# Convolution and expert layer in one kernel: the scatters at a sort's end spread, four tiles kept for them, and one stage with split rows

## The chip, the cores and the metric

One Trainium2 chip, one core. The metric is the device time of one execution in microseconds; the median of three runs is given. A profile of one execution stands beside them.

## The reference

```python
# x: (8, 5696, 128), h: (5696, 128); E = 8 experts, F = 1024
y = irfft(rfft(x, n=2*S, axis=1) * rfft(h, n=2*S, axis=0)[None], n=2*S, axis=1)[:, :S]
x = y.reshape(8 * 5696, 128)
logits = x @ w_gate                       # (45568, 8)
e = argmax(logits); gate = max softmax(logits)
for each expert e:
    out[rows of e] = gate * (relu(x[rows of e] @ w1[e]) @ w2[e])
```

A long convolution over the sequence for every channel, and then for each of 45568 tokens the one expert of eight that scores highest: 128 to 1024, relu, 1024 to 128, times its softmax weight. All in float32.

## The kernel before, in words

**The work.** The convolution is a Fourier transform in two factors (48 and 120 points) written as matmuls, and goes through three groups of batches: group 0 has 2 batches, groups 1 and 2 have 3 each. Each group passes three stages:

- Stage A (`steps_a`, `phase_a`): 120 x 512 blocks of x times a 120-point matrix; the result goes to the DRAM tensor U. With `A3[g]` true the rows are split first: `cut` makes a rounded copy on ScalarE (line 258) and the remainder on the engine that `ALO[g]` names (line 259), and each transform is three matmuls in the fast float32 kind in place of one in whole float32 (line 280).
- Stage B (`phase_b`), the filter: U by frequency, forward matmul `xp` (line 470), product with the filter on VectorE (495, 498), the sum `combine` (506, on POOL; for group 2's first `ALONE` = 20 steps on VectorE), inverse matmul `vp` (514), copy, store to V. 120 steps for a group.
- Stage C (`phase_c`), the last transform and the sort: `yp` (647) from V, rows to `rt` (662), transposes, logits, the choice of expert (`route`), the rank in its list (`rank`). Every column of 120 tokens then waits in the list `sorts` until `sort_one` sends it with one indirect DMA from POOL to its rows in the DRAM tensor SR (584), at most 8 in flight. 48 steps for group 1 and for group 2, three columns a step.

When a group's sort is done, `tables` works out on VectorE which tiles of 256 rows are complete, and the group's part of the expert layer may start (`moe`): part 0 has 37 tiles, part 1 67, part 2 the rest. A tile is read from SR (940; seven buffers `xr`), weights are read where the expert changes (961), and each of its four steps is layer 1 (992), relu on ScalarE (998) and its remainder on VectorE (1000), two steps later layer 2 (1012). The tile's rows are then delivered by two indirect DMAs from POOL (1035). The first row load of a part waits for the last scatters of its sort.

**The order.** Every engine and DMA queue runs its instructions in the order in which the program issues them. That order comes from generators: each yields a cost in ns, and `run` always continues the one whose sum of costs, divided by its share, is smallest. These costs only set the order. An expert step costs 1420; the rest (`rest`, all stages of groups 1 and 2) has the share 0.75. A filter step of group 2 costs 0.78 x 1280 = 998, a sort step of group 1 `RATE[2]` x 3150, one of group 2 `RATE[5]` x 3150.

While group 1 is sorted, group 2's stage A runs inside it as a guest (72 transforms, up to two for a sort step; `A3[2]` is false). Scatters are taken from `sorts` at `settle`, at `logit_out`, and by each relu of an expert step; whatever is left when the sort ends is sent at once.

A part whose sort had a guest isn't released by the sort, but in the next group's stage B, when that stage's costs exceed `HEAD`:

```python
for cost in phase_b(gr):
    spent += cost
    yield cost
    if spent > HEAD and wait:
        wait.pop().ready = True
```

Group 2's stage B begins with a yield of 6000. While no part is released, `experts` is held and the rest goes on alone.

Of the kernel before, what the change touches and what calls it, by code (L numbers as in the profile page):

```python
# [49 lines left out]
HOLD = (0, 0, 0)  # L50
AHEAD = 2
ALONE = 20
HEAD = 26000
A3 = (True, True, False)
ALO = ('gpsimd', 'vector', 'vector')
AT = 650
WARM = 7
# [2 lines left out]
LULL = (29000, 0.448)  # L60
RARE = 3
XR = 7
RATE = (0.372, 0.559, 0.45, 0.8, 0.78, 0.6)


@with_exitstack
def conv_moe(ctx: ExitStack, tc: tile.TileContext, I, out, B, S, D, E, F, split):
# [68 lines left out]
    for g, nbs in enumerate(split):  # L136
        gr = Group(g, b0, sum(nbs))
# [104 lines left out]
    def steps_a(gr, tag, bufs):  # L242
# [7 lines left out]
        xts, uts, xss = {}, {}, {}  # L250
        split = A3[g]

# [56 lines left out]
    def phase_a(gr):  # L309
        start, begin, store, flush, M = steps_a(gr, "six", SIX)  # L310
        half = AT if gr.g == 0 else 750 * RATE[3 * gr.g - 3]
        start()
# [10 lines left out]
    class Guest:  # L323
# [17 lines left out]
        def rest(self):  # L341
            while self.m < self.M:
                self.begin(2)
                yield 1500 * RATE[3 * self.gr.g - 3]
                self.end()
# [53 lines left out]
    def phase_b(gr):  # L399
# [117 lines left out]
        def save(n):  # L517
            q, c = items[n]
            qb, k0 = divmod(q, QB)
            if k0 == 0 and c == 0:  # L520
                outs_[qb] = sb.tile([K2, QB, gr.cols], F32, tag="six", name=f"vt{g}_{q}", bufs=SIX)
            nc.scalar.copy(outs_[qb][:, k0, c * cw : (c + 1) * cw], banks.pop(n)[:K2, :cw])  # L522
            if k0 == QB - 1 and c == nch - 1:
                late.append((gr.V[qb * QB : qb * QB + QB].rearrange("q p c -> p q c"), outs_.pop(qb)))
                tiles.pop(qb), hhs.pop(qb), mats.pop(qb)
# [18 lines left out]
        for n in range(N + BLAGS[3] + 2):  # L544
# [24 lines left out]
            if 0 <= n - ds_ < N:  # L569
                save(n - ds_)  # L570
            yield max(cw * 7 / 2.4 + 200, 2 * cw / 0.96 + 300) if g == 0 else RATE[3 * g - 2] * cw * 8 / 2.4

# [5 lines left out]
    sorts = []  # L578

    def sort_one(after=None):  # L580
        if not sorts:
            return
        pi, rt, b = sorts.pop(0)
        s = nc.gpsimd.indirect_dma_start(  # L584
            out=SR[:, :],
            out_offset=IndirectOffsetOnAxis(ap=pi[:, b : b + 1], axis=0),
            in_=rt[:, b, :],
            in_offset=None,
            bounds_check=NROWS - 1,
            oob_is_err=False,  # L590
        ).ins
        tc.declare_no_dep(s, group="sr", reason="each row of the sorted tokens is written once, before it is read")
        tc.declare_no_dep(s, group="rows", reason="never a row that a tile has read")
        tc.add_to_no_dep_group("sr", s)
        if len(lanes) >= PIPE_LANES:
            tc.add_manual_dep(s, lanes[-PIPE_LANES].name, SYNC, reason="scatter lane")
        if after is not None:
            tc.add_manual_dep(s, after.name, SYNC, reason="scatters are spread over the stage")
        lanes.append(s)

    def phase_c(pt, guest=None):
        gr, g, nb, cb, cw, NI, ns = pt.gr, pt.s, pt.nb, pt.cb, pt.cw, pt.ni, pt.ns
# [187 lines left out]

        cost = max(2 * cw * 8 / 2.4 + 260 * cb, 1040 * cb) + 150 if g == 0 else RATE[3 * gr.g - 1] * 1050 * cb
        for i in range(2):
# [43 lines left out]
                if at >= total_sub + LL:  # L836
                    break
        while sorts:
            sort_one()

    def tables(pt):
        g, NT, base = pt.s, pt.nt, state["base"]
# [259 lines left out]
    def gather(pt, guest=None):  # L1102
        state["hold"] = HOLD[pt.s]
        yield from phase_c(pt, guest)
        state["hold"] = 0
        tables(pt)
        if pt is parts[-1]:
            yield from fill(pt)
        if guest is None:
            pt.ready = True  # L1110
        yield 0
# [5 lines left out]
    def rest():  # L1117
        yield from phase_a(groups[1])
        wait = []
        for gr in groups[1:]:  # L1120
            spent = 0
# [5 lines that stand above are left out]
# [137 lines left out]
```

## Time and profile before

| | |
|---|---|
| runs | 2358.23 us median (2357.75 to 2363.87) |
| profiled execution | 2359.16 us, its span 2357.3 us |
| mean granted clock of TensorE | 0.944 |
| TensorE matmuls | 2141.5 us busy, 91% |
| VectorE | 1563.4 us, 66% |
| ScalarE | 1089.6 us, 46% |
| GpSimd (POOL) | 1123.6 us, 48%, 1141 instructions |
| expert steps | 728; scatters of sorted rows 384, deliveries 364 |

The span is the time from the first to the last instruction. The granted clock is the share of full speed that TensorE was allowed. Busy times of TensorE are modelled for pipelined matmuls; the pause between two DMA instructions on POOL doesn't count as busy. A row of a group names the line, the engine, the operation, output and inputs, how often it ran, busy us and mean ns, and behind the second bar the idle time of the engine just before it and what ended that.

### The profile page before, as it was taken

The numbers are of one execution on the slowest core, as the hardware profiler recorded it, in microseconds if no ns is written. First come the engines' busy times: TensorE is split into PE (matmuls) and PEld (weight loads), VectorE is DVE, ScalarE is ACT, GpSimd is POOL, SyncE is SP. The second block draws the span as 40 slices with busy tenths as digits, with TensorE's granted clock in tenths as the row PEclk, the third lists the DMA queues.
The fourth block names the chain that finished last, engine by engine and source line by source line (L and its number), as shares of the span: only waits on it lengthen the run. The fifth ranks groups of instructions, "written<-read, shape, count | busy, mean of one in ns | idle before, by whom it ended". The sixth has DMA issues, their size and how long they took to land.

```text
span 2357.3 us, 46665 instructions
## 1 busy us (share of the span) xinstructions
PE 2141.5 (91%) x13998; PEld 1758.2 (75%) x13998; DVE 1563.4 (66%) x3887; ACT 1089.6 (46%) x2353; POOL 1123.6 (48%) x1141
## 2 busy tenths in 40 slices
PE   7899777759999899997899998999879999999997
PEld 4666444437777777774477777998778999999997
DVE  3599843549999556668688885677644455555554
ACT  3666543324344455552244444665434444444443
POOL 4455425735555346675155552577762223333332
PEclk7999989779999999996699999999989999999998
DMA  8999998599999677877779875566332333333331
GB/s 261 302 310 316 286 288 269 157 282 244 237 261 256 183 234 227 245 239 190 189 186 238 211 212 141 120 176 171 87 89 86 110 115 117 112 116 112 116 112 30
DMA packets 230109, 449.87 MB, mean 191 GB/s; under 512 B 32945, under 2 KB 143591, under 8 KB 229856
## 3 DMA queue, kind: packets, MB, share of 16 engines
q1 hardware_dynamic: 205920, 399.77, 59.5%
q0 software_dynamic: 23936, 47.09, 6.7%
q8 instruction: 115, 1.88, 0.3%
q14 instruction: 138, 1.13, 0.2%
HBM read 590.12 MB, written 171.96 MB: 323 GB/s over the span
## 4 chain that ended last, share of the span: by engine, by line
PE 67%; DMA 12%; issue 9%; DVE 5%; POOL 3%; ACT 2%; SPq 2%; POOLq 0%; ACTq 0%; DVEq 0%
PE mh L992 18%; PE ma L1012 17%; PE vp L514 7%; PE xp L470 7%; PE yp L647 5%; PE pa L280 5%; DMA wb<-WD 4%; DMA SR<-rt,pi 3%; PE mx L168 3%; DVE xs L498 2%; PE tp L686 1%; PE tp L168 1%; DMA mt<-mq 1%; POOL out L1035 1%; POOL SR L584 1%
## 5 line engine op out<-in xcount | busy, mean ns | idle before, releaser
L1000 DVE SCALAR_TENSOR_TENSOR hs<-mh,hs 128x512 fp32r<-128x512 f32 x728 | 502.8, 691 | 457.9 <-ACT hs L998 453.7
L992 PE MATMUL mh<-xtb,wb 128*128 128x256 f32 x4368 | 727.6, 302 | 39.6 <-DMA wb<-WD 27.7
L992 PEld LDWEIGHTS mh<-xtb,wb 128*128 128x128 f32 x4368 | 596.0, 192 | 124.5 <-issue 70.7
L1035 POOL DMA_INDIRECT out<-xr x364 | 361.9, 994 | 669.4 <-DVE xr L1026 565.6
L998 ACT ACTIVATE hs<-mh 128x512 fp32r<-128x512 f32 x728 | 435.4, 598 | 506.3 <-PE mh L992 504.1
L1012 PE MATMUL ma<-hs,wb 128*128 128x256 f32 x4368 | 659.3, 287 | 8.4 <-DMA wb<-WD 8.4
L1012 PEld LDWEIGHTS ma<-hs,wb 128*128 128x128 f32 x4368 | 577.3, 192 | 10.5 <-DMA wb<-WD 10.2
L584 POOL DMA_INDIRECT SR<-rt,pi x384 | 399.2, 1040 | 215.6 <-issue 69.5
L506 POOL TENSOR_TENSOR zt<-zt,xs 128x384 f32<-128x384 f32 (+1 forms) x340 | 310.7, 928 | 288.6 <-DVE xs L498 208.6
L498 DVE TENSOR_TENSOR xs<-xp,hh 64x384 f32<-64x384 f32 (+1 forms) x720 | 367.5, 510 | 14.3 <-POOL zt L506 0.9
L522 ACT COPY vt<-vp 96x384 f32<-96x384 f32 (+1 forms) x360 | 158.3, 440 | 430.5 <-PE vp L514 417.1
L470 PE MATMUL xp<-uq,mt 96*128 96x384 f32 (+1 forms) x720 | 289.6, 487 | 33.2 <-DMA uq<-U 14.8
L514 PE MATMUL vp<-zt,mi 128*96 128x384 f32 (+1 forms) x720 | 283.1, 476 | 14.2 <-DVE xs L498 5.0
L495 DVE TENSOR_TENSOR zt<-xp,hh 128x384 f32<-128x384 f32 (+1 forms) x360 | 183.7, 510 | 58.0 <-PE xp L470 36.9
L514 PEld LDWEIGHTS vp<-zt,mi 128*96 128x96 f32 x720 | 113.8, 169 | 127.3 <-issue 76.6
L470 PEld LDWEIGHTS xp<-uq,mt 96*128 96x128 f32 x720 | 121.5, 202 | 77.6 <-issue 34.1
L280 PE MATMUL pa<-xc,fcr 120*120 120x512 f32 x360 | 112.8, 453 | 33.0 <-ACT xc L258 11.3
L647 PE MATMUL yp<-vr,gcr 120*120 120x384 f32 x576 | 116.7, 337 | 0.3 <-DVE vr L635 0.2
L280 PEld LDWEIGHTS pa<-xc,fcr 120*120 120x120 f32 x360 | 69.5, 207 | 60.3 <-ACT xc L258 14.2
L635 DVE TENSOR_TENSOR vr<-vq,vr 120x768 fp32r<-120x768 f32 x96 | 91.7, 957 | 33.4 <-ACT vr L634 32.9
L647 PEld LDWEIGHTS yp<-vr,gcr 120*120 120x120 f32 x576 | 95.9, 182 | 0.8 <-DVE vr L635 0.8
L292 ACT COPY ut<-pa 120x512 f32<-120x512 f32 x96 | 56.2, 585 | 77.1 <-PE pa L280 67.3
(121 smaller groups left out, 2003.5 us busy)
## 6 DMA issues: line engine op xcount, KB each, us to landing
wb<-WD SPq DMA_DIRECT2D x728, 512.0 KB
vq<-V SPq DMA_DIRECT2D x64, 720.0 KB
U<-ut SPq DMA_DIRECT2D x48, 720.0 KB
uq<-U SPq DMA_DIRECT2D x60, 576.0 KB
V<-vt SPq DMA_DIRECT2D x60, 576.0 KB
xr<-SR SPq DMA_DIRECT2D x182, 130.0 KB
xt<-x SPq DMA_DIRECT2D x96, 240.0 KB
hh<-HS SPq DMA_DIRECT2D x120, 192.0 KB
```

What stands on the lines that cost most here:

```text
L280: nc.tensor.matmul(banks[m][:QN, :], lhs, rhs, start=(k == 0), stop=(k == len(ops) - 1))
L470: nc.tensor.matmul(xp[:, :cw], mt[:, k0, :], uc, start=True, stop=True)
L498: nc.vector.tensor_tensor(out=xs[to], in0=x3[at], in1=hv[at, 1].broadcast_to([HP, cb, D]), op=ALU.mult)
L506: eng.tensor_tensor(out=zt, in0=zt, in1=xs, op=ALU.add)
L514: nc.tensor.matmul(vp[:K2, :cw], mi[:, k0, :], zt.rearrange("p b d -> p (b d)"), start=True, stop=True)
L584: s = nc.gpsimd.indirect_dma_start(out=SR[:, :], out_offset=IndirectOffsetOnAxis(ap=pi[:, b : b + 1], axis=0), in_=rt[:, b, :], in_offset= ...
L647: nc.tensor.matmul(yp[:MP, :cw], lhs, rhs, start=(m == 0), stop=(m == len(ops) - 1))
L992: nc.tensor.matmul(hp[:, u, :], wb[:, a, f, :], xt[:, b, :], start=(n == 0), stop=(n == 2))
L998: done = nc.scalar.activation(hs[:, 0], hp, AF.Relu)
L1000: nc.vector.scalar_tensor_tensor(out=hs[:, 1], in0=hp, scalar=0.0, in1=hs[:, 0].bitcast(F32), op0=ALU.max, op1=ALU.subtract)
L1012: nc.tensor.matmul(accs[j], wb[:, a, f, :], hs[:, b, u, :], start=(k == 0 and u == 0 and n == 0), stop=(k == NPAIR - 1 and u == 1 and n == 2),
L1035: sc = nc.gpsimd.indirect_dma_start(out=out[:, :], out_offset=IndirectOffsetOnAxis(ap=xr[:, s, D + 1 : D + 2].bitcast(I32), axis=0), in_=x ...
```

## The change

- `HEAD` 26000 becomes 10000.
- `A3[2]` becomes true: the guest stage (group 2's stage A) splits its rows, with the remainder on VectorE (`ALO[2]`).
- `RATE[2]` 0.45 becomes 0.32: the cost of group 1's sort step.
- At the end of the sort of groups 1 and 2, a scatter that is left is sent only where a yield has passed in which nobody else took one.

```diff
-HEAD = 26000
-A3 = (True, True, False)
+HEAD = 10000
+A3 = (True, True, True)
...
-RATE = (0.372, 0.559, 0.45, 0.8, 0.78, 0.6)
+RATE = (0.372, 0.559, 0.32, 0.8, 0.78, 0.6)
...
         while sorts:
-            sort_one()
+            left = len(sorts)
+            if gr.g:
+                yield cost
+            if len(sorts) == left:
+                sort_one()
```

## The prediction

> **What bounds the kernel now.** I read the page's slices first, to find where TensorE is slow, then the busy table of six stretches, then groups of instructions inside those stretches, and last the timeline at the two places that stand out.
>
> ```profile
> PE   7899777759999899997899998999879999999997
> ...
> PEclk7999989779999999996699999999989999999998
> DMA  8999998599999677877779875566332333333331
> ```
>
> Each digit is a slice of 59 us. The clock falls to 6 in two slices, 1060 to 1180 us, and nowhere else. The next table gives stretches, in us, with each engine's busy time, the granted clock, DMA share and GB/s:
>
> ```profile
> 860.00:1060.00 200.00, 198.38 (x1379) 154.94 (x1378) 131.68 (x510) 111.78 (x268) 140.57 (x137) 1.00 0.80 241
> 1077.00:1156.00 79.00, 59.33 (x86) 22.29 (x86) 58.35 (x139) 8.82 (x19) 24.89 (x25) 0.51 0.71 177
> 1180.00:1400.00 220.00, 218.72 (x1293) 170.96 (x1291) 193.87 (x352) 93.93 (x192) 114.20 (x116) 1.00 0.83 216
> 1500.00:1650.00 150.00, 148.75 (x1243) 135.44 (x1243) 108.88 (x434) 92.56 (x225) 116.93 (x109) 1.00 0.64 164
> 1699.00:1748.00 49.00, 30.81 (x212) 29.86 (x213) 24.72 (x74) 12.39 (x25) 37.69 (x38) 0.82 0.35 102
> 1900.00:2200.00 300.00, 300.00 (x2529) 300.00 (x2528) 166.75 (x293) 146.94 (x292) 94.68 (x98) 1.00 0.39 127
> ```
>
> In order: group 1's sort with the guest stage beside part 0's expert steps; the hole behind it; group 2's filter stage with part 1's steps; group 2's sort; its end; expert steps alone. TensorE is full everywhere but in the hole (clock 0.51, hardly an expert step) and at the second sort's end. The hole in TensorE's timeline:
>
> ```profile
> 1074.31 0.98 PE L1012 MATMUL ma<-hs,wb 128*128 128x256 f32 x6
> ...
> 1153.26 0.63 PE L168 MATMUL mx_None<-ident,xr 128*128 128x128 f32 x2
> 1156.49 1.62 PE L992 MATMUL mh<-xtb,wb 128*128 128x256 f32 x6 [2.60 <-DMA wb<-WD]
> ```
>
> Part 0's last layer ends at 1075.3; part 1's first starts at 1156.5. The 81 us between hold 22 filter steps of group 2, at half clock. Why 22: part 1 is released when the planner has spent more than HEAD in that stage, 6000 + 21 x 998.4 = 26966 > 26000, and one more step goes out before the experts' turn. The scatters were done long before (18 of them, on POOL):
>
> ```profile
> L584 POOL DMA_INDIRECT SR<-rt,pi x18 | 18.4, 1020 | 5.5 <-issue 5.5
> ```
>
> That is the group in 1084 to 1108, and the tables on VectorE end at 1088.8 (row below). So the order holds part 1 back, not the data.
>
> **The change, part by part.**
>
> *Order, by the planner's costs.* A sort step of group 1 costs 0.45 x 3150 = 1418, by its share 0.75 1890, against 1420 for an expert step: 1.33 expert steps each. With 0.32 it is 1344: 0.95. Over 48 steps and four half ones the sort takes 19 expert steps fewer, so it ends 19 steps (16 whole, 3 of the tail) before part 0 does. The new yields cost 1344 for each of the 18 scatters left: one per expert step, and the rest of part 0 covers them. HEAD 10000 is passed at 6000 + 5 x 998.4: 6 filter steps stand ahead of part 1 in place of 22.
>
> *The sort of group 1, 860 to 1060 us.* Its groups, from three answers, on TensorE, on POOL and on VectorE:
>
> ```profile
> L992 PE MATMUL mh<-xtb,wb 128*128 128x256 f32 x294 | 57.5, 331 | 0.3 <-DMA wb<-WD 0.3
> L280 PE MATMUL pa<-xt,c_fcs 120*120 120x512 f32 x112 | 57.4, 618 | 0.0
> L647 PE MATMUL yp<-vr,gcr 120*120 120x384 f32 x222 | 44.8, 337 | 0.0
> L584 POOL DMA_INDIRECT SR<-rt,pi x111 | 114.5, 1031 | 51.8 <-issue 25.7 <-ACT rt L662 4.1 <-DVE wm L745 4.1
> L1035 POOL DMA_INDIRECT out<-xr x26 | 27.7, 1066 | 7.9 <-issue 6.7 <-DVE ut L292 0.9 <-DVE wm L745 0.3
> L635 DVE TENSOR_TENSOR vr<-vq,vr 120x768 fp32r<-120x768 f32 x37 | 35.5, 959 | 24.8 <-ACT vr L634 24.8
> ```
>
> Six L647 make a sort step: 37 of them, 5.41 us each; six L992 an expert step: 49, the forecast 1.33 a step. Expert steps alone cost
>
> ```profile
> L998 ACT ACTIVATE hs<-mh 128x512 fp32r<-128x512 f32 x195 | 116.5, 597 | 147.6 <-PE mh L992 147.6
> ```
>
> 300/195 = 1.54 us (1900 to 2200). So 0.38 steps fewer for each sort step give 0.58 us. Split rows: the chain has both kinds,
>
> ```profile
> 60.94 2.10 PE pa L280 x9
> ...
> 1006.62 1.91 PE pa L280 x4
> ```
>
> three transforms of three split matmuls in 2.10 (0.70 each), two whole ones in 1.91 (0.955): 0.25 saved, 72 transforms, 1.5 a step: 0.38. TensorE would need 5.41 - 0.58 - 0.38 = 4.45 us. But POOL: 3.0 scatters and 0.47 deliveries a step, at (114.5 + 27.7)/137 = 1.04 busy and 0.30 between two (5.5/18 in the row of 18): 3.47 x 1.34 = 4.65. In group 2's sort, where POOL is full, an operation takes 150/109 = 1.38: 4.77. I take 4.7: POOL binds, not TensorE, and eats two thirds of what the split saves. Before the first ranks (six steps) TensorE's 4.5 holds: 42 x 0.71 + 6 x 0.9 = **-35 us**. The added work lies beside that: 36 ScalarE copies, and on VectorE
>
> ```profile
> L259 DVE TENSOR_TENSOR xc<-xt,xc 120x512 fp32r<-120x512 f32 x36 | 24.9, 693 | 65.8 <-ACT xc L258 47.9 <-DMA xt<-x 17.9
> ```
>
> 0.52 us a step on an engine that is 66% busy; were POOL faster by far, TensorE would be late next. DMA moves the same bytes in less time.
>
> *The 19 postponed steps* come behind the sort: 16 x 1.54 + 2 = **+27 us**, now with scatters beside them. POOL has 18 + 6 operations there, 32 us, and stands L behind TensorE at the sort's end: 3 where it keeps abreast, 20 in group 2's sort now (its last step is at 1699 us, the burst that is queued behind it begins at 1719.5, rows below). I take L = 12, in the middle. Queued behind a scatter that waits for its step are the deliveries; who waits for those is the load of the next row tile (seven buffers), so some 20 us of lag cost nothing.
>
> *The hole.* What is late next is the last scatter: 32 + L behind the sort's end, 5 + L behind part 0's end. Then come its landing and part 1's loads, on SP's queue:
>
> ```profile
> 1148.58 3.37 SPq L940 DMA_DIRECT2D xr<-SR  x3
> 1152.75 1.93 SPq L961 DMA_DIRECT2D wb<-WD  x4
> ```
>
> 7.9 us from the first row load to the matmul at 1156.49, and for the scatter 1.0 and
>
> ```profile
> 1739.24 2.35 DMA SR<-rt,pi
> ```
>
> So 5 + 12 + 3.4 + 7.9 = 28 us. The six filter steps and the tables lie inside it:
>
> ```profile
> 1080.00 0.15 DVE L845 TENSOR_TENSOR cnt<-base,c_base 1x8 f32<-1x8 f32 x1
> ...
> 1088.64 0.15 DVE L907 TENSOR_TENSOR did<-did,did 1x8 f32<-1x8 f32 x1
> ```
>
> 8.8 us. Part 1's loads go ahead of the filter's later ones on SP; those are needed only by steps that TensorE reaches afterwards. Bounds: 20 with L = 3, 39 with L = 23. 81 to 28: **-53 us**.
>
> *The 16 filter steps* move beside expert steps. From 1180 to 1400, on TensorE and on ScalarE:
>
> ```profile
> L470 PE MATMUL xp<-uq,mt 96*128 96x384 f32 x160 | 64.7, 485 | 0.0
> L998 ACT ACTIVATE hs<-mh 128x512 fp32r<-128x512 f32 x75 | 44.9, 599 | 18.2 <-PE mh L992 18.2
> ```
>
> 80 filter and 75 expert steps: (220 - 75 x 1.54)/80 = 1.31 us, 16 of them 21 us. Fourteen of these still add on VectorE (n < 20), which has 193.9/80 = 2.4 of 2.75 us taken; with 0.56 more it binds by 0.2 a step, 3 us. **+24 us**.
>
> *The second sort's end.* 14 scatters, which the yields spread over 14 expert steps.
>
> Expert steps and scatters there, 1699 to 1748 and 1719.5 to 1741.6 us:
>
> ```profile
> L998 ACT ACTIVATE hs<-mh 128x512 fp32r<-128x512 f32 x17 | 10.1, 597 | 29.9 <-PE mh L992 29.9
> ```
>
> ```profile
> L584 POOL DMA_INDIRECT SR<-rt,pi x17 | 16.9, 997 | 5.2 <-issue 4.9 <-DMA SR<-rt,pi 0.3
> ```
>
> and TensorE's two longest waits:
>
> ```profile
> 1716.67 1.65 PE L992 MATMUL mh<-xtb,wb 128*128 128x256 f32 x6 [5.72 <-DVE hs L1000]
> ...
> 1747.61 1.62 PE L992 MATMUL mh<-xtb,wb 128*128 128x256 f32 x6 [5.62 <-DMA wb<-WD]
> ```
>
> 17 steps in 49 us where 26 are due. The stall before 1716 is VectorE busy with the tables: it stays, 14 steps later. That before 1747 follows the burst of 17 scatters on POOL, 22 us: deliveries stood behind it, so a row load, so the weights queued behind that on SP. Spread, POOL has 14 scatters and 7 deliveries in 14 steps, 28 us against 22: the lag grows by 6 instead of 18. Between 0 and 12 us; I take **-6**. Part 1 has 12 expert steps left when part 2 is ready (41 before): that cover shrinks, but holds.
>
> Sum: 2359.16 (the profiled execution; its span is 2357.3) - 35 + 27 - 53 + 24 - 6 = 2316. The median of the runs is 0.9 lower: 2315.
>
> *A rule against the change.* Added cuts read two operands in SBUF on VectorE, as L635 does. Beside L635 a scatter takes 1.031 on the mean, in the burst 0.997: 0.034 x 137 = 5 us lost on 35.5 us of such work, so the cuts' 25 us cost 3 to 4, inside my 4.7. The Trainium skill, SBUF — State Buffer, "Who interferes with whom", says that a VectorE instruction with two SBUF inputs contends with a GpSimd one that reads SBUF, and that the second waits for the first in full; it also infers that descriptor generation is spared. Rows of this case agree with the sparing. By the full lock the sum would be that of the third rival.
>
> **The rivals.**
> - *POOL doesn't bind.* TensorE's 4.5 holds, L stays 3, the hole is 20, the end gives 12: -42 + 27 - 61 + 24 - 12: 2295. For it: POOL's pitch in the burst is 1.30. Against: group 2's sort runs at 1.38.
> - *The scatters come late.* The sort gains only 14 us, L reaches the ring's 23, the hole is 40, the end gives nothing: -14 + 27 - 41 + 24: 2355, no change. For it: the 20 us at the end of group 2's sort.
> - *VectorE's cuts hold POOL up.* All 0.52 us a step: 4.65 + 0.52 = 5.17, the sort gains 15, and L is larger by 8: 2359 - 15 + 27 - 45 + 24 - 6 = 2344. Against: the 0.034 above.
> - *Slower: the denser sort runs into DMA.* A sort step takes 0.80 x 5.41 = 4.3 us of all queues' time, 4.1 with fewer expert steps, 0.87 of 4.7. If transfers so packed held a step at 5.6 or more, 0.9 x 48 eats all the gain; at 6.0, 62 us lost, 2378. Against: between 590 and 770 us the DMA slices show nines and TensorE's too.
>
> **How the numbers follow.** Forecast 0.58 (2302 to 2332), POOL free 0.15, late scatters 0.10, cuts 0.10, DMA 0.07. Leaving out the slower case, the late one's upper half and a little below the free one: 2294 to 2348. 0.3% is 7 us, 2351 to 2365, about what a measurement of this kernel can tell from no change. Faster: 0.58 + 0.15 + 0.10 + 0.04 of the late case = 0.87; same 0.06; slower 0.07.
>
> **What would show it.** The clock slices near 1060 to 1180 should read 8 or 9; part 0's last to part 1's first matmul some 28 us, its wait on row loads behind scatters; sort steps of group 1 at 4.7 us with POOL near 1.35 us an operation without pause; 576 split transforms' matmuls in place of 144 whole ones plus 360; one scatter between two relus at both sorts' ends. I am wrong if POOL pauses in that sort (then it is less), if a scatter beside the cuts lasts 1.2 us, or if the hole's end waits for something not named here, such as the filter's own steps.

## The result and the profile after

The changed kernel takes 2305.65 us (median of 4 runs, 2302.67 to 2308.33) against 2361.05 us for the kernel before (4 runs): a ratio of 0.9766, interval 0.9747 to 0.9785. Measured again in another round it was 2305.38 against 2357.18: 0.9787, 0.9766 to 0.9807. The profiled execution's span is 2300.9 us, 56.4 less than before, and TensorE's mean granted clock is 0.958 (0.944 before). One execution of all those below, the profiled one of *changed*, took 2999.89 us at a granted clock of 0.645; it is left out of its ratio, and its trace is not read. Behind line 839 every line number is 4 larger than before: layer 1 is L996, layer 2 L1016, the relu L1002, the row load L944, the weight load L965, the delivery L1039.

The page's slices of the changed kernel, 57.5 us each:

```profile
PE   6899878759999999997899999999979999999997
...
PEclk8999979779999999999899999999989999999999
DMA  8999999599999779966787875656523333333330
```

Where the clock read 6 in two slices, one reads 8, for 1093 to 1150 us. The table of stretches shows the sort with the guest, the part behind that sort, the hole, the filter, group 2's sort, its end, and expert steps alone:

```profile
850.00:1000.00 150.00, 142.76 (x1040) 120.31 (x1038) 113.72 (x432) 97.08 (x229) 118.62 (x104) 0.98 0.89 263
1044.00:1077.00 33.00, 30.20 (x232) 29.23 (x232) 19.10 (x56) 13.39 (x27) 25.38 (x26) 0.95 0.47 137
1077.00:1102.00 25.00, 10.03 (x20) 3.89 (x20) 20.33 (x51) 1.25 (x4) 12.66 (x13) 0.67 0.85 222
1180.00:1400.00 220.00, 218.89 (x1291) 170.87 (x1290) 193.98 (x353) 93.34 (x192) 116.33 (x118) 1.00 0.84 221
1500.00:1650.00 150.00, 147.62 (x1240) 134.75 (x1238) 108.39 (x426) 91.81 (x223) 115.88 (x113) 1.00 0.62 158
1681.00:1798.00 117.00, 101.90 (x804) 99.93 (x804) 63.29 (x141) 46.09 (x91) 60.85 (x61) 0.94 0.27 78
1900.00:2200.00 300.00, 300.00 (x2529) 300.00 (x2529) 166.53 (x292) 146.83 (x291) 95.40 (x98) 1.00 0.39 126
```

In filter, second sort and steps alone each engine's busy time is as before to within 2%. The sort with the guest isn't full of TensorE any more (95%), and the hole is some 25 us. The second sort's end is fuller: 87% of 117 us, where the kernel before has 79% of the 117 us from the same mark (the 49 us shown in the prediction, 63%, are its worst part):

```profile
1699.00:1816.00 117.00, 92.71 (x691) 91.06 (x692) 55.60 (x128) 40.22 (x80) 57.52 (x59) 0.88 0.31 94
```

TensorE's timeline at the changed kernel's hole:

```profile
1074.19 2.43 PE L1016 MATMUL ma<-hs,wb 128*128 128x256 f32 x18
...
1078.32 2.82 PE L470 MATMUL xp<-uq,mt 96*128 96x384 f32 x8 [0.80 <-DMA uq<-U]
1086.65 1.62 PE L470 MATMUL xp<-uq,mt 96*128 96x384 f32 x2 [5.51 <-DVE xs L498]
...
1097.00 0.69 PE L168 MATMUL mx_None<-ident,xr 128*128 128x128 f32 x2 [3.36 <-DMA xr<-SR]
1102.29 1.62 PE L996 MATMUL mh<-xtb,wb 128*128 128x256 f32 x6 [4.61 <-DMA wb<-WD]
```

And on POOL and SP (SPq: SP's queue of loads and stores), with the last scatter at 1089.56 and the row loads that it lets go:

```profile
1089.56 1.01 POOL L584 DMA_INDIRECT SR<-rt,pi  x1 [0.30 <-issue]
```

```profile
1094.87 2.73 SPq L944 DMA_DIRECT2D xr<-SR  x3
1098.37 2.09 SPq L965 DMA_DIRECT2D wb<-WD  x4
```

Part 0's last layer ends at 1076.6, the last scatter starts 13.0 us later, the row load is issued 5.3 behind it, and part 1's first layer starts 7.4 later: 25.7 us. The six filter steps ahead of part 1 are done before the rows come.

The same marks taken from the timelines of five kernels (the last three are experiments, below) split the time from group 1's sort on. Each mark is the start of a matmul, part 0's end the end of one:

| us | before | changed | HEAD 26000 | RATE 0.45 | guest whole |
|---|---|---|---|---|---|
| a: group 1's sort, first L647 to last L711 | 268.2 | 240.1 | 241.5 | 262.8 | 240.9 |
| b: to part 0's last layer | -1.8 | 32.1 | 31.8 | -1.8 | 30.6 |
| c: the hole, to part 1's first layer | 81.2 | 25.7 | 76.0 | 43.6 | 25.0 |
| d: to group 2's last inverse transform, L514 | 278.3 | 324.1 | 278.7 | 324.7 | 324.9 |
| e: to the end of group 2's sort | 264.5 | 254.7 | 266.1 | 251.8 | 253.0 |
| f: to part 1's last transposes but one, L168 | 149.6 | 112.8 | 143.4 | 113.7 | 112.5 |
| a + b + c | 347.6 | 297.9 | 349.3 | 304.6 | 296.5 |

The changed kernel gains 50.5 of its 56.4 us in a to f; 4.5 lie ahead of a, in unchanged code, and 1.4 behind f. The 4.5 say nothing of the change: the same mark lies anywhere from 798.8 to 810.1 us in the six profiles on chips like the first.

### The profile page after: what moved, and what is told of

Its sections match the earlier page's. It is cut to its first block, busy times and chain, and to the rows that moved or that the text cites. A ratio compares the mean times of both kernels' runs of the same rounds, so it can differ in the third digit from the quotient of the medians.

```text
span 2300.9 us, 46887 instructions
## 1 busy us (share of the span) xinstructions
PE 2104.2 (91%) x14070; PEld 1760.2 (77%) x14070; DVE 1584.7 (69%) x3923; ACT 1110.2 (48%) x2389; POOL 1133.3 (49%) x1141
## 4 chain that ended last, share of the span: by engine, by line
PE 68%; DMA 12%; issue 8%; DVE 4%; POOL 3%; ACT 2%; SPq 2%; POOLq 0%; DVEq 0%; ACTq 0%
PE mh L996 19%; PE ma L1016 18%; PE vp L514 8%; PE xp L470 7%; DMA SR<-rt,pi 4%; PE yp L647 4%; PE pa L280 3%; PE mx L168 3%; DMA wb<-WD 3%; PE tp L686 1%; PE tp L168 1%; DVE xs L498 1%; POOL out L1039 1%; DMA xt<-x 1%; DMA U<-ut 1%
## 5 line engine op out<-in xcount | busy, mean ns | idle before, releaser
L996 PE MATMUL mh<-xtb,wb 128*128 128x256 f32 x4368 | 710.8, 298 | 25.2 <-DMA wb<-WD 14.1
L1039 POOL DMA_INDIRECT out<-xr x364 | 363.6, 999 | 677.7 <-DVE xr L1030 563.7
L996 PEld LDWEIGHTS mh<-xtb,wb 128*128 128x128 f32 x4368 | 594.4, 191 | 97.1 <-issue 43.1
L1016 PE MATMUL ma<-hs,wb 128*128 128x256 f32 x4368 | 657.2, 287 | 6.3 <-DMA wb<-WD 6.3
L1002 ACT ACTIVATE hs<-mh 128x512 fp32r<-128x512 f32 x728 | 435.5, 598 | 441.5 <-PE mh L996 438.0
L1016 PEld LDWEIGHTS ma<-hs,wb 128*128 128x128 f32 x4368 | 575.5, 191 | 8.2 <-DMA wb<-WD 7.9
L584 POOL DMA_INDIRECT SR<-rt,pi x384 | 407.3, 1061 | 195.3 <-DMA xt<-x 62.6
L470 PE MATMUL xp<-uq,mt 96*128 96x384 f32 (+1 forms) x720 | 274.3, 464 | 20.3 <-DMA uq<-U 13.3
L514 PE MATMUL vp<-zt,mi 128*96 128x384 f32 (+1 forms) x720 | 273.9, 462 | 17.5 <-DVE xs L498 5.7
L280 PE MATMUL pa<-xc,fcr 120*120 120x512 f32 x576 | 179.6, 447 | 38.3 <-ACT xc L258 15.6
L514 PEld LDWEIGHTS vp<-zt,mi 128*96 128x96 f32 x720 | 108.3, 164 | 131.6 <-issue 76.9
L280 PEld LDWEIGHTS pa<-xc,fcr 120*120 120x120 f32 x576 | 106.8, 201 | 79.2 <-ACT xc L258 18.4
L647 PE MATMUL yp<-vr,gcr 120*120 120x384 f32 x576 | 117.2, 338 | 2.1 <-ACT vr L634 0.9
L635 DVE TENSOR_TENSOR vr<-vq,vr 120x768 fp32r<-120x768 f32 x96 | 91.6, 956 | 33.4 <-ACT vr L634 32.8
L259 DVE TENSOR_TENSOR xc<-xt,xc 120x512 fp32r<-120x512 f32 x72 | 49.7, 692 | 77.2 <-ACT xc L258 76.8
L647 PEld LDWEIGHTS yp<-vr,gcr 120*120 120x120 f32 x576 | 96.3, 183 | 3.3 <-ACT ut L292 1.1
```

The lines of the kernel that those rows point to most:

```text
L280: nc.tensor.matmul(banks[m][:QN, :], lhs, rhs, start=(k == 0), stop=(k == len(ops) - 1))
L470: nc.tensor.matmul(xp[:, :cw], mt[:, k0, :], uc, start=True, stop=True)
L514: nc.tensor.matmul(vp[:K2, :cw], mi[:, k0, :], zt.rearrange("p b d -> p (b d)"), start=True, stop=True)
L584: s = nc.gpsimd.indirect_dma_start(out=SR[:, :], out_offset=IndirectOffsetOnAxis(ap=pi[:, b : b + 1], axis=0), in_=rt[:, b, :], in_offset= ...
L647: nc.tensor.matmul(yp[:MP, :cw], lhs, rhs, start=(m == 0), stop=(m == len(ops) - 1))
L996: nc.tensor.matmul(hp[:, u, :], wb[:, a, f, :], xt[:, b, :], start=(n == 0), stop=(n == 2))
```

## The experiments

The theory: the hole was held by the written order (HEAD), and once that is lifted by POOL's last scatter; the other three edits only shape what stands beside it. The rivals were that the denser sort (split and RATE) brings the gain, that the yields do, and that the cuts on VectorE hold POOL up.

The first eight runs fell on two other chips, where the kernel before takes 2506 and 2500 us: the sort of group 1 takes 287 to 298 us there in the kernels that differ from the changed one in one thing, with TensorE idle for 43 to 53 us of it and POOL for 49 to 58 us beyond its 0.30 between two operations. Only ratios and differences within a set are read there, not microseconds against the first chip; numbers of microseconds in their expectations were written for the first chip.

**On the second chip: one edit alone, or one left out.**

*head_alone*, the kernel before with

```diff
-HEAD = 26000
+HEAD = 10000
```

> The kernel before with HEAD 10000 and nothing else. By my account the hole then ends some 12 us behind the last scatter of the burst (1106.4 in the run before): 44 us of hole in place of 81, and 16 filter steps come back beside expert steps at 1.4 us each, so -37 + 23 = -14 us, and up to 10 less where the expert changes fall luckier: 2337 to 2347. Rival: HEAD alone made the hole and the kept tiles only shift work; the hole is then near 26 us as in the changed kernel, and the time 2320 to 2330.

Measured: 0.9916 (0.9890 to 0.9942) of the kernel before, 21 us of 2506. Its hole, from part 0's last layer to part 1's first, is 40 us and ends 9.7 us behind the last scatter (1177.12), as the account had it (44 and 12) and not the rival (26); the transposes wait for rows:

```profile
1181.78 0.69 PE L168 MATMUL mx_None<-ident,xr 128*128 128x128 f32 x2 [12.26 <-DMA xr<-SR]
```

*no_split*, the changed kernel with

```diff
-A3 = (True, True, True)
+A3 = (True, True, False)
```

> The changed kernel with the guest stage in whole rows again. If POOL's queue sets the sort's pace (104 operations in 150 us, a scatter 1.14 us on the mean), the split saves TensorE nothing that shows: scatters fall back to 1.03 us, the sort step stays at 4.8 to 4.9 us, and the time is 2303 to 2311. If TensorE's work counted, its 18 us come back: 2320 to 2325.

Measured: 0.9904 (0.9869 to 0.9938).

*one_input*, the changed kernel with a plain copy in place of the guest's remainder (the remainder is left out of the computation):

```diff
-            getattr(nc, ALO[g]).tensor_tensor(out=xs[:, 1], in0=xt, in1=xs[:, 0].bitcast(F32), op=ALU.subtract)
+            if g == 2:
+                nc.vector.tensor_copy(xs[:, 1], xt)
+            else:
+                getattr(nc, ALO[g]).tensor_tensor(out=xs[:, 1], in0=xt, in1=xs[:, 0].bitcast(F32), op=ALU.subtract)
```

> The changed kernel with the guest stage's remainder replaced by a rounded copy of the row: the second input of that VectorE instruction and the remainder's value are left out. If scatters that start beside the cut wait for VectorE's second input, those of 1.4 us go back to 1.0, the mean of the sort's scatters falls from 1.14 to about 1.07, the sort step from 4.84 to about 4.6, the time by 8 to 14 us to 2292 to 2298. If scatters are longer because the sort is denser (DMA), they stay at 1.14 and the time at 2302 to 2309.

Measured: 0.9898 (0.9862 to 0.9935).

*spread_first*, the changed kernel with yields at the first sort's end alone:

```diff
-            if gr.g:
+            if gr.g == 1:
```

> The changed kernel with the yields at the end of group 1's sort alone; group 2's last 14 scatters go at once again. If spreading them is what made the second sort's end cheaper (14 us less lost than before), most of that comes back: 2315 to 2320. If it came from part 1 standing 15 steps further and from where its experts change, nothing moves: 2302 to 2309.

Measured: 0.9895 (0.9861 to 0.9929). The four intervals overlap throughout, so HEAD alone can't be told here from the three with everything but one part; the changed kernel itself was not run on this chip. The traces tell a little more. The hole is 17 to 19 us in the last three. In group 1's sort the mean of the 144 scatters is 1.062 us with the cuts (*spread_first*), 1.041 with the copy (*one_input*) and 1.041 without the split (*no_split*). And stretch f is 124.7 us without the yields in the second sort, 121.1 and 122.7 with them: 2 to 4 us, not the 14 of the expectation (one profile each).

**On the third chip: the changed kernel with one more alteration each.**

*changed*:

> The changed kernel itself, unaltered, so that the others have it beside them on the same chip. On the chip of its first runs it took 0.977 of the kernel before. Where a chip takes longer in the sorts' transfers than there, both theories expect a ratio nearer to 1 (0.98 to 0.99), since three of its four parts shorten stages in which TensorE waited for its own work or for nothing, not for transfers. The hole between part 0's last and part 1's first matmul: 20 to 45 us.

Measured: 0.9877 (0.9853 to 0.9900). Its hole is not known.

*no_spread*, without the yield:

```diff
             left = len(sorts)
-            if gr.g:
-                yield cost
             if len(sorts) == left:
```

> The changed kernel without the yield: whatever scatters are left at a sort's end go at once, the other three parts stay. In the written order the filter then begins 13 expert steps before part 0's end and part 1 is released before that end. Theory A, the last scatter sets the hole's end: it is issued some 19 expert steps (about 30 us) earlier while POOL's backlog is the same, so the hole shrinks from about 26 us to under 10; the second sort's end loses 6 to 14 us by the burst; together 0 to 10 us below the changed kernel. Theory B, the yields are what makes the gain (a burst holds deliveries, row loads and weights up): 10 us or more above the changed kernel, with stalls of 5 us on weights behind the burst.

Measured: 0.9933 (0.9908 to 0.9957), 0.0056 +- 0.0034 or 14 +- 8 us above the changed kernel. Theory A has the hole right and its price wrong. The last scatter came 17 us earlier than with the yields (1141.69 against 1158.76 in the copy's run below, their sorts starting within 0.4 us), and the hole is 7.6 us against 16.5 there. But it saves nothing: from the sort's start to the last filter step 14 us are gained, and nine expert steps fewer are done, which cost the same 14 us later. Group 2's sort and its end then take 6 us each more than those steps explain. TensorE's waits in that end, 1780 to 1860 us (here layer 1 is L994 and the relu's remainder L1002):

```profile
PE mh L994 <- DVE dr L915: 8.2, 1, 8.2
PE gb L168 <- ACT lt L700: 5.8, 1, 5.8
PE mh L994 <- DVE hs L1002: 5.5, 1, 5.5
```

The longest wait stands behind the tables (L915 is the copy that follows them on VectorE), not on weights behind the burst, as theory B had it. That the yields are worth something on that chip is shown; by which wait is not.

*rate_025*:

```diff
-RATE = (0.372, 0.559, 0.32, 0.8, 0.78, 0.6)
+RATE = (0.372, 0.559, 0.25, 0.8, 0.78, 0.6)
```

> The changed kernel with a sort step of group 1 costed at 0.25 in place of 0.32 x 3150: about ten more expert steps are left behind the sort. In the written order part 1 is released some five expert steps before part 0's end. Theory A (the hole is what is still to be had, ended by the last scatter): hole under 10 us, the sort itself shorter by the expert steps that move out of it, 10 to 20 us below the changed kernel. Theory B (POOL or the transfers bind the denser sort at its present pace): the sort keeps its time, the postponed steps come on top, and the sum is within 5 us of the changed kernel or above it.

Measured: 0.9940 (0.9919 to 0.9961), 16 +- 8 us above the changed kernel: theory B or worse. Its hole is 7.6 us, as theory A had it, but the sort doesn't shrink with the ten expert steps that leave it: 287.1 us against 293.1 in the copy's run below, where ten steps are 15 us. The steps behind it take 86.5 us in place of 45.6.

*one_input_b*, the copy again:

> The changed kernel with the guest's remainder on VectorE replaced by a copy of the rows (one input from SBUF in place of two; the remainder is left out of the computation). Theory A, two inputs from SBUF hold POOL's descriptor work up: scatters in group 1's sort fall from a mean of 1.14 to 1.05 us or less and the sort of 240 us shortens by 48 x 3 x 0.1 = 14 us, if POOL binds there; 10 to 15 us below the changed kernel. Theory B, they don't, or POOL doesn't bind: within 5 us of the changed kernel.

Measured: 0.9883 (0.9852 to 0.9914), within 10 us of the changed kernel: theory B for the time. But POOL's scatters in that sort, 863 us on, first without the yields (cuts as in the changed kernel) and then with the copy (where the scatter is L587):

```profile
L584 POOL DMA_INDIRECT SR<-rt,pi x115 | 124.6, 1084 | 97.1 <-ACT rt L662 34.3 <-issue 20.2 <-ACT hs L1000 16.4
```

```profile
L587 POOL DMA_INDIRECT SR<-rt,pi x116 | 123.6, 1065 | 101.6 <-ACT rt L665 36.3 <-issue 21.9 <-ACT hs L1005 18.9
```

Of those 115 scatters 22 lasted over 1.2 us, of the 116 with the copy 8. So the second input does lengthen scatters, and where POOL is idle 102 us beside 124 us of them (some 35 of it the 0.30 between two) this costs nothing.

**On a chip like the first** (before: 2357.18 us, 17 runs), each edit taken back by itself.

*changed_b*:

> The changed kernel itself once more, as the measure for the three beside it. From the runs of its kind so far both theories expect 0.977 of the kernel before where the scatters land as on the first chip, and 0.985 to 0.990 where the sorts are slowed by their transfers.

Measured: 2305.38 us, 0.9787 (0.9766 to 0.9807).

*head_back*:

```diff
-HEAD = 10000
+HEAD = 26000
```

> The changed kernel with HEAD 26000 again: part 1 is released 16 filter steps later. Theory A, the earlier release is the largest part by itself (the prediction's terms: 53 us of hole less 24 us of the same filter steps beside expert steps): 29 us above the changed kernel, between 20 and 40, with a hole of 65 to 90 us. Theory B, the postponed expert steps close the hole by themselves and the release adds little: within 10 us of the changed kernel, hole under 40 us.

Measured: 2349.25 us, 0.9969 (0.9959 to 0.9980); 43 +- 6 us above the changed kernel, theory A and some more. With part 1 released late, the other three edits together are worth 8 us. What HEAD alone is worth on this chip was not run. Its hole on TensorE, the last scatter on POOL, and the row loads on SP:

```profile
1072.77 2.43 PE L1016 MATMUL ma<-hs,wb 128*128 128x256 f32 x18
...
1146.57 0.38 PE L168 MATMUL mx_None<-ident,xr 128*128 128x128 f32 x2
1151.22 1.62 PE L996 MATMUL mh<-xtb,wb 128*128 128x256 f32 x6 [4.27 <-DMA wb<-WD]
```

```profile
1087.41 1.01 POOL L584 DMA_INDIRECT SR<-rt,pi  x1 [0.30 <-issue]
```

```profile
1143.07 3.20 SPq L944 DMA_DIRECT2D xr<-SR  x3
```

The last scatter started 59 us before the transposes that need it. The row loads stand behind the filter's loads in SP's queue and go out 56 us after that scatter, and the transposes wait for nothing: here the order holds part 1.

*rate_045*:

```diff
-RATE = (0.372, 0.559, 0.32, 0.8, 0.78, 0.6)
+RATE = (0.372, 0.559, 0.45, 0.8, 0.78, 0.6)
```

> The changed kernel with a sort step of group 1 costed at 0.45 x 3150 again: 19 expert steps go back from behind the sort into it. Theory A, the postponed steps are only moved where they cost what they cost before, and their worth is that they cover the last scatter's landing: the hole grows from 26 to 40 us or more, part 0's end comes with the sort's end, and the sum is 5 to 20 us above the changed kernel. Theory B, the sort is bound by its own transfers and the steps fit into it for nothing: equal to the changed kernel within 5 us or below it.

Measured: 2305.38 us, 0.9795 (0.9773 to 0.9817); 2 +- 7 us above the changed kernel. By the time theory B holds; by the hole theory A does:

```profile
1061.45 0.98 PE L1016 MATMUL ma<-hs,wb 128*128 128x256 f32 x6
...
1100.86 0.69 PE L168 MATMUL mx_None<-ident,xr 128*128 128x128 f32 x2 [15.94 <-DMA xr<-SR]
1106.07 1.62 PE L996 MATMUL mh<-xtb,wb 128*128 128x256 f32 x6 [4.52 <-DMA wb<-WD]
```

```profile
1096.19 1.00 POOL L584 DMA_INDIRECT SR<-rt,pi  x1 [0.30 <-issue]
```

The transposes wait 15.9 us for rows that the last scatter, 34 us behind part 0's end, lets go. The sort is 23 us longer than in the changed kernel, the hole 18, and the 34 us of postponed steps behind the sort are gone (a, b, c in the table): 304.6 against 297.9. What the two orders have in common is POOL: the last scatter starts 285 us behind the sort's first matmul in the changed kernel and 295 here, although the sort's matmuls end at 240 and 263.

*no_split_b*, the guest's transforms whole again, as in *no_split*:

> The changed kernel with the guest's transforms whole again (A3[2] false). Theory A, TensorE's time in the sort is what the split saves: (624 - 3 x 148) ns x 144 = 26 us if TensorE binds, and with it half of that or more is seen: 13 to 26 us above the changed kernel. Theory B, the sort is held by POOL or by the scatters' landing, and TensorE only waits more: within 8 us of the changed kernel, TensorE's busy share of the sort 3 to 5 points lower in the changed kernel than here.

Measured: 2304.68 us, 0.9787 (0.9768 to 0.9806): no difference, +- 7 us. Its sort, its transforms and its scatters:

```profile
845.00:995.00 150.00, 148.30 (x997) 110.89 (x995) 101.67 (x417) 85.64 (x207) 109.12 (x106) 1.00 0.87 268
```

```profile
L280 PE MATMUL pa<-xt,c_fcs 120*120 120x512 f32 x95 | 49.8, 621 | 1.0 <-DVE rk L773 1.0
L647 PE MATMUL yp<-vr,gcr 120*120 120x384 f32 x186 | 38.1, 340 | 0.7 <-ACT ut L292 0.7
```

```profile
L584 POOL DMA_INDIRECT SR<-rt,pi x144 | 147.9, 1027 | 71.4 <-issue 41.0 <-ACT rt L662 12.0 <-ACT hs L1002 4.6
```

The changed kernel's rows for the same, 850 to 1000 us and all 144 scatters:

```profile
L280 PE MATMUL pa<-xc,fcr 120*120 120x512 f32 x138 | 42.8, 430 | 1.4 <-DVE rk L773 0.9
L647 PE MATMUL yp<-vr,gcr 120*120 120x384 f32 x186 | 37.6, 337 | 0.7 <-ACT ut L292 0.7
```

```profile
L584 POOL DMA_INDIRECT SR<-rt,pi x144 | 159.3, 1106 | 59.8 <-issue 18.0 <-DMA xt<-x 16.3 <-DMA SR<-rt,pi 4.6
```

Both do 31 sort steps in 150 us, 4.84 each. Whole, TensorE is 99% busy and binds, POOL 73%. Split, TensorE is 95% busy, and POOL has its 104 operations in 118.6 us of work and some 0.30 between two: 104 x 1.44 = 150. The split takes 0.18 us of a step from TensorE (148.30 - 142.76 over 31 steps), and each of a step's three scatters is longer: by 0.079 us on the mean of all 144, by 0.115 in 850 to 1000 us (1.143 against 1.028). The bound changes engines, the step doesn't.

## Why the prediction came out where it did

Forecast 2315, measured 2305.65: the mechanism holds, as head_back shows, but that the sum came so near is in part luck. The sort and the postponed steps together gained 14 us less than forecast; the second sort's end gained 8 more, 10 us came in a place that was left out, and 6 of the profiles' 56.4 us lie outside all stretches that the forecast counts.

- **The hole, -53: measured -55.5** (81.2 to 25.7). Its working holds step by step: the last scatter 13 us behind part 0's end (17 forecast) and 12.7 from there to the first layer (11.3). L, which was taken as 12 from the middle of its bounds, came out at 13: the last scatter starts 45 us behind the sort's end, 32 + 13. head_back shows that HEAD is what lifts the order; rate_045 shows that POOL's last scatter sets the hole that is left.
- **The filter steps, +24: measured +23.** Stretch d is 45.8 us longer and holds 15 expert steps more (111 relus against 96): 45.8 - 15 x 1.54.
- **The sort of group 1, -35: measured -28.** Two sizes were wrong in it. The split's saving on TensorE was taken as 0.25 us a transform, from nine matmuls in a row in one place and four in another. In this sort layer 1 stands behind the transforms, and what counts is the time from their start to layer 1's successor. Two transforms, split (the changed kernel) and whole (no_split_b), where both have the same neighbours:

```profile
918.73 1.64 PE L280 MATMUL pa<-xc,fcr 120*120 120x512 f32 x6
920.21 0.88 PE L996 MATMUL mh<-xtb,wb 128*128 128x256 f32 x6
920.93 0.38 PE L168 MATMUL mx<-ident,ot 128*128 128x128 f32 x2
```

```profile
915.69 1.98 PE L280 MATMUL pa<-xt,c_fcs 120*120 120x512 f32 x4
917.10 1.28 PE L996 MATMUL mh<-xtb,wb 128*128 128x256 f32 x6
918.22 0.38 PE L168 MATMUL mx<-ident,ot 128*128 128x128 f32 x2
```

That is 1.48 + 0.72 split and 1.41 + 1.12 whole, 0.33 saved by two; a single transform takes 0.76 + 0.71 and 0.48 + 1.11, 0.12 saved. Other places differ from these; over 150 us TensorE's busy time fell by 0.18 a step, half of the 0.38 forecast. And an operation of POOL was taken at 1.04 us, where a scatter took 1.14 in 850 to 1000 us, so that POOL's step came to 4.84 and not 4.7. The forecast's own numbers had the sort without the split at 5.41 - 0.58 = 4.83 us a step; no_split_b measured 4.84. At this RATE all of the -28 comes without the split too; at 0.45 the split alone shortens the sort by 5 (262.8 against 268.2, one profile each).
- **The postponed steps, +27: measured +34** (stretch b), so that sort and steps together gave +6 where -8 was forecast. head_back says the same from the other side: with the sort denser but part 1 released late, a + b + c is 349.3 against 347.6.
- **The second sort's end, -6: measured -14.** Stretch f holds 75 expert steps before and 60 after; beyond 1.54 us each it loses 34.1 and 20.4 us. In head_back, where the yields act and part 1 isn't earlier, 75 steps lose 27.9: about half of the gain, 6 us, goes with the yields. These are single profiles, and the changed kernel's second one loses 23.1, so 3 us in it aren't shown. There was more to gain than the forecast counted: of the 49 us in its table 32 steps of 1.54 were due, not 26. The wait before 1747 for weights behind the burst (5.62) is gone; the tables' wait stays, 7.02 us before 1720.69, with the tables on VectorE from 1710.92 to 1719.77.
- **Left out: -10 in stretch e.** Before, TensorE waited for weights between filter and sort,

```profile
1453.07 1.62 PE L992 MATMUL mh<-xtb,wb 128*128 128x256 f32 x6 [6.98 <-DMA wb<-WD]
```

and head_back has the same wait (8.07), while the changed kernel has none there. With part 1 fifteen steps further on, the place where the expert changes lies elsewhere. It is a gain of place; that a release at another step would not have it is argued and was not run.

**The rule that was weighed.** I wrote that the rows agree that descriptor work is spared the lock, because scatters beside L635 lay 0.034 us above those of the burst. That step failed. The 1.031 us was the mean of all 111 scatters of the stretch, and most of them don't meet L635 at all; the few that do are hidden in it. The rows of POOL and VectorE in the changed kernel's second profile show single ones, beside L635 (the remainder of V's rows, in every version) and L259 (the cut):

```profile
909.35 1.51 POOL L584 DMA_INDIRECT SR<-rt,pi  x1 [0.30 <-ACT yt L678]
...
913.77 1.00 POOL L584 DMA_INDIRECT SR<-rt,pi  x1 [0.30 <-issue]
...
922.49 1.78 POOL L584 DMA_INDIRECT SR<-rt,pi  x1 [0.30 <-issue]
```

```profile
909.04 0.95 DVE L635 TENSOR_TENSOR vr<-vq,vr 120x768 fp32r<-120x768 f32 x1
909.91 0.69 DVE L259 TENSOR_TENSOR xc<-xt,xc 120x512 fp32r<-120x512 f32 x1
...
913.90 0.96 DVE L635 TENSOR_TENSOR vr<-vq,vr 120x768 fp32r<-120x768 f32 x1 [2.03 <-ACT vr L634]
...
922.43 0.95 DVE L635 TENSOR_TENSOR vr<-vq,vr 120x768 fp32r<-120x768 f32 x1
```

The scatter at 922.49 starts 0.06 us into an L635 that has 0.89 left, and lasts 0.78 more than the usual 1.00. That at 909.35 starts where L635 has 0.64 left and lasts 0.51 more; the cut that begins during it adds nothing. At 913.77, with L635 starting 0.13 behind it, nothing is lost. So a scatter that starts beside such an instruction lasts longer by what that one has left, less 0.13, and not at all longer where less than that is left. In the changed kernel's first profile this holds to 0.03 us for the 31 scatters that start at least 0.05 us into L635 or a cut; 5 more start within 0.05 us of its beginning and lose nothing, and the other 108 take 1.004 on the mean, none over 1.2. The Trainium skill, SBUF — State Buffer, "Who interferes with whom", has a VectorE instruction with two SBUF inputs contend with a GpSimd one that reads SBUF, and infers that descriptor generation is spared. The first agrees with these rows and with the copy's 8 long scatters in place of 22; the inference does not.

Of the 144 scatters 26 lasted over 1.2 us, the sign of being wrong that the prediction names; in no_split_b 7 did. But the cuts' own price was small: the 11 scatters that start beside a cut lose 3.3 us in all, far from the third rival's 0.52 us a step. The prediction counted 3 to 4, by luck, since its mean had nothing to do with how they are lost. The 25 beside L635 lose 11.5 us, the 16 in no_split_b 3.0. L635 runs in both kernels; with the split the scatters start earlier in it. All four profiles with the split on chips like the first lose 9 to 12 us there, the two without it 3.0 and 3.5; why the starts move so is not shown.

**The rivals.** That POOL doesn't bind is out for the split (no pause on POOL beyond 0.30 in nearly all of 850 to 1000 us), though its time, 2295, lies about as near as the forecast's. Late scatters did not come: the last one lies 13 us behind part 0's end, not 5 + 23. POOL's scatters were held up by 3 x 0.115 = 0.35 us a step, two thirds of the third rival's price, but mostly beside L635 and not by the cuts. Denser DMA (0.89 of all queues' time in the sort, 0.87 forecast) held no step at 5.6.

**A better version** did not show: the changed kernel without the split is equal to it within 7 us, and with one setting of RATE on either side it is equal (0.45) or slower on the chip where that was run (0.25).

## What to carry to other kernels

When an order is written ahead of time, find the resource whose finishing time stays put however the order is shuffled: here POOL's last scatter came 282 to 298 us after the sort began in all five kernels of the table, with 17 expert steps moved and the sort's matmuls ending up to 28 us apart. Of the 52 us gained 43 go when the one edit is taken back that lets part 1 start as soon as that scatter has landed. Where two engines are within a few per cent of binding, a change that takes work from one and lengthens the other's instructions can be worth nothing, as here; write both sums before counting the first. Don't judge an interference by a stretch's mean: take the instructions that overlap, one by one. And price an instruction by the time to the next one on its engine in the place where it will stand, with what follows it there, not by the length of an isolated run of them.

## What the runs showed of the hardware

- A scatter issued from POOL lasts 1.00 us alone. When it starts while L635 or a cut, VectorE instructions with two SBUF inputs, is under way, it lasts longer by what that one has left less 0.13 us, up to 1.79 in all (changed kernel, within 0.03 us for 31 scatters; those that start within 0.05 us of its beginning lose nothing). Over 144 scatters the mean went from 1.027 (no_split_b) to 1.106 us (changed).
- A whole float32 transform delays the matmul behind it: layer 1 takes 1.11 us to its successor after it and 0.71 after a split one, so that the row's busy time puts part of the cost on the wrong line.
- Between chips the same kernel differed by 6% (2357 and 2500 us), and what an edit was worth differed with it: the whole change gave 0.9787 on one and 0.9877 on another.
